# TensorE's instructions in the program's own order from step 40 of 128 on, and the last row tile of the last block in two PSUM banks

## The chip, the cores and the metric

The kernel runs on one core of one Trainium2 chip. The metric is the device time of one execution in microseconds (us). Engines are named as in the profile: PE is TensorE (PEld its weight loads), DVE is VectorE, ACT is ScalarE, POOL is GpSimd, SP issues most DMAs.

## The reference, cut to what matters

Input is a decayed linear attention over 2 sequences of 768 tokens with 8 heads of 64. Its output `x` (2 x 768 x 512) goes through two MLPs:

```python
X = fft(fft(x, axis=1), axis=2)
u = x + real(X)
un = (u - mean(u)) / sqrt(var(u) + 1e-6)
y = u + maximum(un @ w_ch1, 0) @ w_ch2          # 512 -> 2048 -> 512
yn = (y - mean(y)) / sqrt(var(y) + 1e-6) * g_ln
out = y + maximum(yn @ w2_ch1, 0) @ w2_ch2      # the second MLP, other weights
```

## The kernel before, in words

All matrix products of the two MLPs run in fp16 with every operand split into a high and a low part, three matmuls for one (`PASS`: high by high, high by low, low by high). Tokens are worked in four blocks of 384 (three row tiles of 128); the MLP's inner width 2048 in 16 slices of 128, called f. A **step** is one f of one block of one MLP: 128 steps, first MLP blocks 0, 1, 2, 3, second MLP blocks 0, 1, 3, 2. Step 40 is f = 8 of the first MLP's third block.

**One pair of steps** (`mlp_up_fast`, L800 to L855) computes two f at once by seven products of six matmuls with 192 columns (a Strassen-like scheme) into two PSUM banks, `ps_1...` (left) and `ps_2...` (right). I number them: products 1 to 3 in the even step (1 and 2 into the left bank, 3 into the right one), products 4 and 5 (left bank) in the odd step, products 6 (left) and 7 (right) at the end of the odd step (`rest`). Between them stand other engines' steps. After product 2, ACT copies m1 out (`s`, L831) and DVE adds it to product 2 (`s`, L832); product 4 writes the bank that this add reads, so it waits for it. After product 5, DVE forms u3 (`t`, L839) and adds it to the right bank (L840); products 6 and 7 follow. After them DVE adds (L845, L846), ACT makes the high half of `h` (L851) and DVE its low half (L852).

**The down pass** of step n works on f of step n - 3 (`mlp_down`, L877): for each of three row tiles j, three matmuls of 512 columns into a bank `ps_y` that collects all 16 f. In the program's order a pair of steps is: products 1, 2, 3; nine down matmuls; products 4, 5; nine down matmuls (these are the first that need the `h` of the pair before); products 6, 7.

**At the start of a block** products 2 and 3 need `th`, the sums of normalised inputs (`un_sums`, L774): two halves `kk`, each by six DVE adds (L779 to L787), an ACT cast (L794, high) and a POOL subtraction (L795, low). They are issued three steps and one step before the block, so the second half follows DVE's `t` of the last pair of the block before.

**Beside the products**, from about step 48 to 82, the second MLP's weights are converted (`conv_steps`, L280 to L325). For each of 32 tiles ACT makes `half` (L296) and copies it to a PSUM bank `ps_w` (L297), DVE joins it with the low bits (`wf`, L299), ACT scales by the gain (L320) and casts (L321), POOL subtracts (L323). Sums of these weights (`w1_sums`, L746 to L772: DVE, POOL, ACT, POOL) give `sw`, the operands of products 2, 3, 4, 6 and 7. PSUM has eight banks in three pools: "at" with three (`ps_w` and the right bank), "dn" with three (`ps_y`), "up" with two (the left bank).

**What sets the order.** A scheduler takes the program and decides in which order each engine's queue gets its instructions: it goes by the program's order and by a model of when operands are ready, and moves work forward where an engine would idle. Inside `manual_schedule` an engine's instructions keep the order in which the code issues them. Before, PE is manual in the prologue (up to the first MLP's first steps), and again in the last step (L1120 to L1122) and its end; in between the scheduler orders PE. DVE, ACT, POOL and SP are ordered by the scheduler in both kernels, around PE's order.

**The end** (`down_end`, L866): the last two f of the last block are done row tile by row tile, so that the first two tiles are added (L873) and stored (L874) while PE works on. The third row tile is done by halves of 256 columns, in the same bank: six matmuls for the left half, DVE's add of it, six for the right half.

Of the kernel before, what the change touches and what calls it, by code (L numbers as in the profile page):

```python
# [15 lines left out]
ALU = mybir.AluOpType  # L16
# [3 lines left out]
P = 128  # L20
B, H, S, D = 2, 8, 768, 64
DM, DF = 512, 2048
NCH = S // P
NK = DM // P
NF = DF // P
# [16 lines left out]
YS = 2.0 ** -15  # L42
# [10 lines left out]
EARLY0, GATEN, B1, SPC, DS, DC, DFO, DD, D1S, D2S, AO, YA, NR, NE, LN1, L1, L2, F01, F02, TL, R1, R2, SE, PR1, LAG, UB, FB, NW, MQ, SPL = 11, 8, 6, 2.0, 2.0, 5, 1.0, 0.5, 0.5, 1.0, "aba", "aa", 2, 0, 2, 2.5, 2.5, 16, 4, 3, 1.5, 2, "dddd_dppp", 0, 3, 3, 13, 11, 1, 3  # L53

SUMS = {(1, 0): 16, (1, 1): 18, (2, 0): 20, (2, 1): 25, (3, 0): 35, (3, 1): 38, (0, 0): 41, (0, 1): 43}

AWAY = {0: 37, 2: 39, 4: 41, 6: 43, 8: 45, 10: 47}

# [66 lines left out]
def tile_retention_fourier_mlp(ctx: ExitStack, tc: tile.TileContext, a: dict, out: bass.AP):  # L125
    nc = tc.nc
    pe, act, dve, pool, sp = nc.tensor, nc.scalar, nc.vector, nc.gpsimd, nc.sync
# [18 lines left out]
    def bank(which, name):  # L146
        return banks[which].tile([P, 512], F32, tag=which, name=name)

    def f32t(name, spare=None):
        if spare is not None:  # L150
            return wpool.tile([P, 512], F32, tag=f"w2_{spare}", name=name)
        return fp.tile([P, 512], F32, tag="f", name=name)
# [33 lines left out]
    U = [[ut[b][:, j] for j in range(6)] for b in range(B)]  # L186
# [16 lines left out]
    last = mask[:, :, 1:2].rearrange("p h one -> p (h one)")  # L203
# [653 lines left out]

    dn = {}

    def down_mm(m, blk, f, j, c=slice(0, DM)):  # L860
        h, w = hts[m, blk, f], w2t[m, f]
        for n, (x, y) in enumerate(PASS):
            pe.matmul(dn[blk][j][:, c], h[:, x, j * P:(j + 1) * P], w[:, y, c], start=f == 0 and n == 0,  # L863
                      stop=(f == NF - 1 or j == 2 and f == NF - 3) and n == 2, skip_group_check=j == 2)

    def down_end(m, blk):  # L866
        b, mir = divmod(blk, 2)
        for j in range(3):
            o = f32t(f"o{blk}_{j}")
            for c, eng in (((slice(0, DM), sp),) if j < 2 else ((slice(0, DM // 2), sp), (slice(DM // 2, DM), act))):  # L870
                for f in (NF - 2, NF - 1):
                    down_mm(m, blk, f, j, c)
                dve.scalar_tensor_tensor(o[:, c], dn[blk][j][:, c], YS, U[b][mir * 3 + j][:, c], op0=ALU.mult, op1=ALU.add)  # L873
                eng.dma_start(out[b, j * P:(j + 1) * P, c], o[:, c])  # L874

    def mlp_down(m, blk, f):
        if f == 0:  # L877
            dn[blk] = [bank("dn", f"ps_y{m}_{blk}_{j}") for j in range(3)]
        for j in range(3):
            down_mm(m, blk, f, j)  # L880
        if f < NF - 1:
            return
        b, mir = divmod(blk, 2)
        for j in range(3):
            u = U[b][mir * 3 + j]
            if m == 0:
                dve.scalar_tensor_tensor(u, dn[blk][j], YS, u, op0=ALU.mult, op1=ALU.add)  # L887
                continue
            o = f32t(f"o{blk}_{j}")
            dve.scalar_tensor_tensor(o, dn[blk][j], YS, u, op0=ALU.mult, op1=ALU.add)  # L890
            if not mir:
                sp.dma_start(out[b, j * P:(j + 1) * P, :], o)
                continue
            od = dram.tile([P, DM], F32, name=f"od{blk}_{j}")
            sp.dma_start(od, o)
            n0 = 1 if j == 0 else 0
            if n0:
                sp.dma_start(out[b, TB:TB + 1, :], od[0:1])
            ov, iv = out[b], od[:]
            hw = DM // 2  # L900
            sp.dma_start(bass.AP(ov.tensor, ov.offset + (S - P * j - n0) * DM, [[hw, 2], [-DM, P - n0], [1, hw]]),
                         bass.AP(iv.tensor, iv.offset + n0 * DM, [[hw, 2], [DM, P - n0], [1, hw]]))
# [83 lines left out]
    with tc.manual_schedule(engines={mybir.EngineType.PE, mybir.EngineType.DVE, mybir.EngineType.Pool, mybir.EngineType.Activation}):  # L986
        for z in ORDER.split():
# [3 lines left out]
            if z[0] == "W":  # L991
                ps = bank("up", f"warm{len(warm)}")
# [11 lines left out]
    def after(i, task):  # L1004
        with tc.issue_after(gates[i]):
            task()
# [9 lines left out]
    total = 2 * NB * NF  # L1016
    bg = {}
# [23 lines left out]
    n = t + DC + DFO  # L1041
# [46 lines left out]
    def step(n):  # L1088
        m = n // (NB * NF)
        return m, order[m][n // NF % NB], n % NF  # L1090
# [3 lines left out]
    for (m, blk), f in fast_from.items():  # L1094
        for kk in range(2):
            if m == 0 and blk < 3:
                put(16 * blk + f / 2 + kk - 3, lambda blk=blk, kk=kk: un_sums(0, blk, kk))
            else:
                at = m * NB * NF + order[m].index(blk) * NF
                put(at - TL + 2 * kk if (m, blk) != (1, 0) else at - 7 + 2 * kk, lambda m=m, blk=blk, kk=kk: un_sums(m, blk, kk))  # L1100
    for (g, kk), n in SUMS.items():
        put(n, lambda g=g, kk=kk: w1_sums(0, g, kk))

    def unit(n):
        rest = None
        if n < total:
            m, blk, f = step(n)
            if n >= SPL:
                rest = (mlp_up if f < fast_from.get((m, blk), NF) else mlp_up_fast)(m, blk, f)
        for _, _, task in sorted(bg.pop(n, ()), key=lambda z: z[0]):  # L1110
            after("dve", task) if n < GATEN else task()
        if n >= LAG:
            mlp_down(*step(n - LAG))
        if rest:
            rest()

    for n in range(total - 1):
        unit(n)
    assert not bg
    with tc.manual_schedule(engines={mybir.EngineType.PE}):  # L1120
        unit(total - 1)
        mlp_down(*step(total - LAG))  # L1122
        down_end(*step(total - 1)[:2])

# [24 lines left out]
```

## Time and profile before

| | |
|---|---|
| median of 3 runs | 590.84 us (590.81 to 591.52) |
| the profiled execution | 591.02 us, of which the span of its instructions is 589.2 |
| granted TensorE clock over the span | 0.999 |
| PE | busy 569.0 us (97% of the span), 4635 matmuls |
| DVE | 389.3 us (66%) |
| POOL | 280.9 us (48%) |
| ACT | 276.6 us (47%) |
| chain of work that ended last | PE 72%, DVE 10%, DMA 5%, ACT 5%, POOL 4%, issue 3% |

A matmul's duration in the profile holds its way through the array; matmuls follow each other closer than that, so the rate is read from start to start. Idle time of PE counts from the end of such a duration.

### The profile page before, as it was taken

What the parts mean: (1) busy time and instruction counts of PE and PEld (TensorE: products, weight loads), DVE (VectorE), ACT (ScalarE), POOL (GpSimd) and SP (SyncE); (2) the same over time, 40 slices, a digit from 0 to 9 for tenths busy, and PEclk for the clock granted to TensorE, in tenths of its full rate; (3) what the DMA queues carried; (4) which work ended last, traced back from release to release, by engine and by line L of the source; (5) the groups of instructions that cost most, each with busy time, mean ns of one, the idle gap of its engine ahead of it and who ended that gap; (6) DMA issues with size and microseconds to landing.
All of it is one profiled execution on the core that took longest, in us unless ns stands there. A gap on an engine that the chain in (4) does not pass through costs nothing.

```text
span 589.2 us, 11835 instructions
## 1 busy us (share of the span) xinstructions
PE 569.0 (97%) x4635; PEld 375.3 (64%) x4635; DVE 389.3 (66%) x870; ACT 276.6 (47%) x557; POOL 280.9 (48%) x294
## 2 busy tenths in 40 slices
PE   6889999999999999999999999999999999999997
PEld 4745645666554555666766676766767677767774
DVE  6898898667876449678777768766536453555333
ACT  3645789653233333465587787953223132322110
POOL 8925889976543564364466876953112100110000
PEclk9999999999999999999999999999999999999999
DMA  8995269861000011243265452500110025002001
GB/s 282 410 410 192 90 196 315 310 200 36 1 1 0 13 34 27 72 126 108 78 207 157 145 168 82 169 19 2 64 28 19 1 87 57 19 1 87 22 2 54
DMA packets 46470, 63.23 MB, mean 107 GB/s; under 512 B 26192, under 2 KB 28622, under 8 KB 46414
## 3 DMA queue, kind: packets, MB, share of 16 engines
q1 hardware_dynamic: 45598, 62.27, 33.4%
q8 instruction: 36, 0.59, 0.4%
q10 hardware_dynamic: 816, 0.21, 0.2%
q14 instruction: 20, 0.16, 0.1%
HBM read 52.23 MB, written 6.29 MB: 99 GB/s over the span
## 4 chain that ended last, share of the span: by engine, by line
PE 72%; DVE 10%; DMA 5%; ACT 5%; POOL 4%; issue 3%; SPq 0%; DVEq 0%; ACTq 0%; POOLq 0%
PE ps_y L863 35%; PE ps L819 22%; PE ps_h L726 10%; DMA kt<-in_kt 3%; POOL w L323 2%; PE ps_d L536 1%; DMA cdsd<-in_cd 1%; PE ps_s L361 1%; DMA u<-in_w 1%; ACT w L321 1%; DVE wr L759 1%; PE ps_i L403 1%; DVE u L887 1%; POOL sw L771 1%; ACT wf L320 1%
## 5 line engine op out<-in xcount | busy, mean ns | idle before, releaser
L863 PE MATMUL ps_y<-w,h 128*128 128x512 f16 x1158 | 280.3, 378 | 3.8 <-ACT h L851 1.6
L863 PEld LDWEIGHTS <-h 128*128 128x128 f16 x1158 | 109.4, 98 | 103.7 <-issue 4.5
L819 PEld LDWEIGHTS <-sw 128*128 128x128 f16 x1104 | 94.5, 98 | 17.0 <-issue 2.6
L819 PE MATMUL ps<-th,sw 128*128 128x192 f16 x828 | 92.0, 246 | 1.0 <-DVE wf L299 0.7
L819 PEld LDWEIGHTS <-w 128*128 128x128 f16 x828 | 71.9, 98 | 18.7 <-issue 0.2
L323 POOL TENSOR_TENSOR w<-wf,w 128x512 f16<-128x512 f32 x58 | 66.9, 1162 | 27.6 <-ACT w L321 27.5
L851 ACT ACTIVATE h<-ps 128x384 f16<-128x384 f32 x92 | 43.5, 489 | 71.7 <-DVE ps L845 67.3
L726 PE MATMUL ps_h<-unT,w 128*128 128x384 f16 x396 | 71.6, 326 | 0.1
L819 PE MATMUL ps<-unT,w 128*128 128x192 f16 x552 | 62.4, 246 | 0.0
L852 DVE SCALAR_TENSOR_TENSOR h<-ps,h 128x384 f16<-128x384 f32 x92 | 49.1, 554 | 14.2 <-ACT h L851 12.7
L726 PEld LDWEIGHTS <-w 128*128 128x128 f16 x396 | 37.9, 98 | 28.2 <-issue 0.5
L839 DVE TENSOR_TENSOR t<-ps,s 128x192 f32<-128x192 f32 x46 | 16.3, 354 | 51.1 <-PE ps L819 51.1
L771 POOL TENSOR_TENSOR sw<-ws,sw 128x512 f16<-128x512 f32 x32 | 37.3, 1182 | 20.8 <-ACT sw L770 20.8
L689 POOL TENSOR_TENSOR uns<-un,uns 128x512 f16<-128x512 f32 x21 | 25.2, 1201 | 39.6 <-ACT uns L688 39.6
L831 ACT COPY s<-ps 128x192 f32<-128x192 f32 x46 | 14.5, 315 | 61.5 <-PE ps L819 61.4
L668 POOL TENSOR_TENSOR rs<-rs,neghalf 128x1 f32<-128x1 f32 x24 | 14.3, 601 | 59.2 <-DVE rs L666 58.8
L321 ACT CAST w<-wf 128x512 f16<-128x512 f32 x58 | 35.2, 613 | 11.9 <-DVE wf L308 9.4
L795 POOL TENSOR_TENSOR th<-ts,th 128x384 f16<-128x384 f32 x24 | 22.1, 938 | 38.8 <-ACT th L794 38.8
L373 POOL TENSOR_TENSOR m<-m,m 128x512 f16<-128x512 f32 x24 | 31.6, 1335 | 4.3 <-ACT m L371 4.2
L845 DVE TENSOR_TENSOR ps<-ps,s 128x192 f32<-128x192 f32 x46 | 16.5, 360 | 25.2 <-PE ps L819 25.0
L741 DVE SCALAR_TENSOR_TENSOR h<-ps_h,h 128x384 f16<-128x384 f32 x36 | 19.8, 552 | 20.1 <-ACT h L740 20.0
L299 DVE SCALAR_TENSOR_TENSOR wf<-ws,ps_w 128x512 int32<-128x512 int32 x32 | 21.9, 686 | 14.8 <-ACT ps_w L297 8.8
(167 smaller groups left out, 834.4 us busy)
## 6 DMA issues: line engine op xcount, KB each, us to landing
ws<-in_w SPq DMA_DIRECT2D x25, 511.8 KB, 3.3
ws<-in_w2b SPq DMA_DIRECT2D x16, 511.8 KB, 4.0
ws<-in_w1b SPq DMA_DIRECT2D x16, 511.8 KB, 4.0
kt<-in_kt SPq DMA_DIRECT2D x12, 256.0 KB, 5.8
qt<-in_qt SPq DMA_DIRECT2D x12, 256.0 KB, 5.2
v<-in_v SPq DMA_DIRECT2D x12, 256.0 KB
k<-in_k SPq DMA_DIRECT2D x12, 256.0 KB, 5.1
pre<-in_w SPq DMA_DIRECT2D x4, 511.8 KB
```

The costliest lines, as they stand in the source:

```text
L299: dve.scalar_tensor_tensor(ti, raw[:, :, 0], 13, part.bitcast(I32), op0=ALU.logical_shift_right, op1=ALU.bitwise_or)
L321: act.copy(hi, t)
L323: (dve if m == 0 and i in (LD1 if kind == 1 else LD2) else pool).tensor_tensor(lo, t, hi, op=ALU.subtract)
L373: pool.tensor_tensor(t[:, 1], m32, t[:, 0], op=ALU.subtract)
L689: pool.tensor_tensor(s_[:, 1], un, s_[:, 0], op=ALU.subtract)
L726: pe.matmul(ps, w[:, i, k, fo:fo + P], x[:, j, k, :], start=n == 0, stop=n == 11)
L771: pool.tensor_tensor(lo, z, hi, op=ALU.subtract)
L795: pool.tensor_tensor(t[:, 1], z, t[:, 0], op=ALU.subtract)
L819: pe.matmul(ps, lhs, rhs, start=start and n == 0, stop=n == 5, skip_group_check=True)
L851: gate["relu"] = act.activation(hi, z, AF.Relu)
L852: dve.scalar_tensor_tensor(lo, z, 0.0, hi, op0=ALU.max, op1=ALU.subtract)
L863: pe.matmul(dn[blk][j][:, c], h[:, x, j * P:(j + 1) * P], w[:, y, c], start=f == 0 and n == 0, stop=(f == NF - 1 or j == 2 and f == NF - 3 ...
```

## The change

From step 40 on (`HAND`) all steps are issued inside `manual_schedule` for PE, so that PE's queue has the program's order up to the end. In the last block (second MLP, block 2) the third row tile gets two accumulators of 256 columns for the whole block, one in a bank of pool "dn" and one in a bank of pool "at"; each down pass of that block then has three matmuls of 256 columns for either instead of three of 512. `down_end` goes through the same list of parts. Nothing else is added or removed.

```diff
--- before.py
+++ after.py
@@ -53,6 +53,8 @@
 
+
+HAND = 40
 
 
@@ -857,37 +859,42 @@
 
     dn = {}
 
-    def down_mm(m, blk, f, j, c=slice(0, DM)):
+    WHOLE, LEFT, RIGHT = slice(0, DM), slice(0, DM // 2), slice(DM // 2, DM)
+
+    def down_mm(m, blk, f, part):
+        j, c, ps = part
         h, w = hts[m, blk, f], w2t[m, f]
         for n, (x, y) in enumerate(PASS):
-            pe.matmul(dn[blk][j][:, c], h[:, x, j * P:(j + 1) * P], w[:, y, c], start=f == 0 and n == 0,
-                      stop=(f == NF - 1 or j == 2 and f == NF - 3) and n == 2, skip_group_check=j == 2)
+            pe.matmul(ps, h[:, x, j * P:(j + 1) * P], w[:, y, c], start=f == 0 and n == 0, stop=f == NF - 1 and n == 2)
 
     def down_end(m, blk):
         b, mir = divmod(blk, 2)
-        for j in range(3):
-            o = f32t(f"o{blk}_{j}")
-            for c, eng in (((slice(0, DM), sp),) if j < 2 else ((slice(0, DM // 2), sp), (slice(DM // 2, DM), act))):
-                for f in (NF - 2, NF - 1):
-                    down_mm(m, blk, f, j, c)
-                dve.scalar_tensor_tensor(o[:, c], dn[blk][j][:, c], YS, U[b][mir * 3 + j][:, c], op0=ALU.mult, op1=ALU.add)
-                eng.dma_start(out[b, j * P:(j + 1) * P, c], o[:, c])
+        o = [f32t(f"o{blk}_{j}") for j in range(3)]
+        for part in dn[blk]:
+            j, c, ps = part
+            for f in (NF - 2, NF - 1):
+                down_mm(m, blk, f, part)
+            dve.scalar_tensor_tensor(o[j][:, c], ps, YS, U[b][mir * 3 + j][:, c], op0=ALU.mult, op1=ALU.add)
+            (act if c == RIGHT else sp).dma_start(out[b, j * P:(j + 1) * P, c], o[j][:, c])
 
     def mlp_down(m, blk, f):
         if f == 0:
-            dn[blk] = [bank("dn", f"ps_y{m}_{blk}_{j}") for j in range(3)]
-        for j in range(3):
-            down_mm(m, blk, f, j)
+            last = (m, blk) == step(total - 1)[:2]
+            dn[blk] = [(j, WHOLE, bank("dn", f"ps_y{m}_{blk}_{j}")) for j in range(2 if last else 3)]
+            if last:
+                dn[blk] += [(2, c, bank(z, f"ps_y{m}_{blk}_{z}")[:, :DM // 2]) for c, z in ((LEFT, "dn"), (RIGHT, "at"))]
+        for part in dn[blk]:
+            down_mm(m, blk, f, part)
         if f < NF - 1:
             return
         b, mir = divmod(blk, 2)
-        for j in range(3):
+        for j, _, ps in dn[blk]:
             u = U[b][mir * 3 + j]
             if m == 0:
-                dve.scalar_tensor_tensor(u, dn[blk][j], YS, u, op0=ALU.mult, op1=ALU.add)
+                dve.scalar_tensor_tensor(u, ps, YS, u, op0=ALU.mult, op1=ALU.add)
                 continue
             o = f32t(f"o{blk}_{j}")
-            dve.scalar_tensor_tensor(o, dn[blk][j], YS, u, op0=ALU.mult, op1=ALU.add)
+            dve.scalar_tensor_tensor(o, ps, YS, u, op0=ALU.mult, op1=ALU.add)
             if not mir:
                 sp.dma_start(out[b, j * P:(j + 1) * P, :], o)
                 continue
@@ -1114,11 +1121,12 @@
         if rest:
             rest()
 
-    for n in range(total - 1):
+    for n in range(HAND):
         unit(n)
-    assert not bg
     with tc.manual_schedule(engines={mybir.EngineType.PE}):
-        unit(total - 1)
+        for n in range(HAND, total):
+            unit(n)
+        assert not bg
         mlp_down(*step(total - LAG))
         down_end(*step(total - 1)[:2])
 
```

The tiles below carry the program's names and a number; line numbers of the changed kernel are two higher up to L857. First PE, at the start of the second MLP's third block (block 3); `ps_11_3_0` is the left bank of its first pair, `th0_1_3_0` and `th0_1_3_1` are the two halves of the sums, `ps_y1_1_0` is the down pass of the block before. Before:

```order
L819 MATMUL ps_11_3_0_6289<-unT1_3_5817,w1_1_0_4071 128x192
L819 LDWEIGHTS sw1_0_0_4110
L819 MATMUL ps_11_3_0_6289<-th0_1_3_0_6163,sw1_0_0_4110 128x192
L863 LDWEIGHTS h1_1_6_6192
L863 MATMUL ps_y1_1_0_5729<-w2_1_13_5454,h1_1_6_6192 128x512
```

With the change:

```order
L821 MATMUL ps_11_3_0_6291<-unT1_3_5819,w1_1_0_4073 128x192
L821 LDWEIGHTS sw1_0_0_4112
L821 MATMUL ps_11_3_0_6291<-th0_1_3_0_6165,sw1_0_0_4112 128x192
L821 LDWEIGHTS sw1_0_1_0_4284
L821 MATMUL ps_11_3_0_6291<-th0_1_3_1_6256,sw1_0_1_0_4284 128x192
```

What moved: product 2 is no longer broken off after its first matmul; its second one, which reads the second half of the sums, stands right behind.

Second DVE, between the pairs f = 6 and f = 8 of the first MLP's last block (block 3); `wf` are conversions, `h0_3_3` is what the pair f = 6 gives, `s0_3_8` and `t0_3_9` belong to the pair f = 8. Before:

```order
L840 TENSOR_TENSOR ps_20_3_6_4162<-ps_20_3_6_4162,t0_3_7_4204 128x192
L299 SCALAR_TENSOR_TENSOR wf2_1_3_4336<-ws2_1_3_4334,ps_w2_1_3_4338 128x512
L764 TENSOR_TENSOR ws12_1_0_1_4284<-wf1_1_1_4209,wf1_1_3_4273 128x256
L832 TENSOR_TENSOR s0_3_8_4248<-ps_10_3_8_4249,s0_3_8_4248 128x192
L845 TENSOR_TENSOR ps_10_3_6_4161<-ps_10_3_6_4161,s0_3_6_4160 128x192
L846 TENSOR_TENSOR ps_20_3_6_4162<-ps_20_3_6_4162,s0_3_6_4160 128x192
L852 SCALAR_TENSOR_TENSOR h0_3_3_4243<-ps_10_3_6_4161,h0_3_3_4243 128x2x192
L852 SCALAR_TENSOR_TENSOR h0_3_3_4243<-ps_20_3_6_4162,h0_3_3_4243 128x2x192
L299 SCALAR_TENSOR_TENSOR wf1_1_4_4398<-ws1_1_4_4396,ps_w1_1_4_4400 128x512
L839 TENSOR_TENSOR t0_3_9_4315<-ps_10_3_8_4249,s0_3_8_4248 128x192
```

With the change:

```order
L847 TENSOR_TENSOR ps_10_3_6_4163<-ps_10_3_6_4163,s0_3_6_4162 128x192
L301 SCALAR_TENSOR_TENSOR wf1_1_3_4275<-ws1_1_3_4273,ps_w1_1_3_4277 128x512
L848 TENSOR_TENSOR ps_20_3_6_4164<-ps_20_3_6_4164,s0_3_6_4162 128x192
L854 SCALAR_TENSOR_TENSOR h0_3_3_4245<-ps_10_3_6_4163,h0_3_3_4245 128x2x192
L766 TENSOR_TENSOR ws12_1_0_1_4286<-wf1_1_1_4211,wf1_1_3_4275 128x256
L301 SCALAR_TENSOR_TENSOR wf2_1_3_4338<-ws2_1_3_4336,ps_w2_1_3_4340 128x512
L834 TENSOR_TENSOR s0_3_8_4250<-ps_10_3_8_4251,s0_3_8_4250 128x192
L854 SCALAR_TENSOR_TENSOR h0_3_3_4245<-ps_20_3_6_4164,h0_3_3_4245 128x2x192
L841 TENSOR_TENSOR t0_3_9_4317<-ps_10_3_8_4251,s0_3_8_4250 128x192
```

What moved: the adds of the pair f = 6 and its left `h` stand ahead of `s0_3_8`, which now follows them and both conversions.

Third ACT, at the same block's pair f = 10, whose copy is `s0_3_10`; `h0_3_4` is what the pair f = 8 gives. Before:

```order
L321 CAST w1_1_1_4404<-wf1_1_4_4398 128x512
L296 ACTIVATE half2_1_5_4562<-ws2_1_5_4559 128x512
L831 COPY s0_3_10_4373<-ps_10_3_10_4374 128x192
L320 ACTIVATE wf1_1_6_4452<-wf1_1_6_4452,gcol_187 128x512
L794 CAST th0_1_0_0_4328<-ts12_1_0_0_4322 128x384
L321 CAST w1_1_1_4404<-wf1_1_6_4452 128x512
L794 CAST th1_1_0_0_4331<-ts34_1_0_0_4323 128x384
L851 ACTIVATE h0_3_4_4368<-ps_10_3_8_4249 128x2x192
L851 ACTIVATE h0_3_4_4368<-ps_20_3_8_4250 128x2x192
L297 CAST ps_w1_1_5_4552<-half1_1_5_4551 128x512
```

With the change:

```order
L299 CAST ps_w1_1_4_4402<-half1_1_4_4401 128x512
L796 CAST th0_1_0_0_4330<-ts12_1_0_0_4324 128x384
L853 ACTIVATE h0_3_4_4370<-ps_10_3_8_4251 128x2x192
L298 ACTIVATE half1_1_5_4553<-ws1_1_5_4550 128x512
L796 CAST th1_1_0_0_4333<-ts34_1_0_0_4325 128x384
L322 ACTIVATE wf1_1_4_4400<-wf1_1_4_4400,gcol_187 128x512
L299 CAST ps_w1_1_6_4456<-half1_1_6_4455 128x512
L833 COPY s0_3_10_4375<-ps_10_3_10_4376 128x192
L853 ACTIVATE h0_3_4_4370<-ps_20_3_8_4252 128x2x192
L323 CAST w1_1_1_4406<-wf1_1_4_4400 128x512
```

What moved: the two activations of `h0_3_4` stood behind `s0_3_10` and four steps of conversions and sums that follow it; now the left one stands ahead of `s0_3_10`, with four such steps between them, and the right one just behind it.

## Rows read from the trace of the kernel before

**Rows 1.** PE groups by form, 251.13 to 586.1 us: busy us, mean ns, idle us before.
```profile
L863 PE MATMUL ps_y<-w,h 128*128 128x512 f16 x815 | 198.9, 379 | 1.2 <-ACT h L851 1.2
L819 PE MATMUL ps<-th,sw 128*128 128x192 f16 x788 | 87.6, 246 | 1.0 <-DVE wf L299 0.7
L819 PE MATMUL ps<-unT,w 128*128 128x192 f16 x522 | 59.1, 246 | 0.0
L819 PE MATMUL ps<-th,w 128*128 128x192 f16 x270 | 30.1, 246 | 0.0
...
L863 PE MATMUL ps_y<-w,h 128*128 128x256 f16 x12 | 1.6, 272 | 0.5 <-DVE o L873 0.5
```

**Rows 2.** Chain that ended last, 571 to 576 us: start us, us, what.
```profile
571.63 2.06 PE ps L819 x25
573.69 1.94 PE ps_y L863 x9
```

**Rows 3.** Windows, PE alone: stretch, its length, busy us (count), granted clock, DMA.
```profile
280.00:340.00 60.00, 58.39 (x477) 1.00 0.49 149
340.00:400.00 60.00, 59.44 (x484) 1.00 0.35 103
400.00:580.00 180.00, 179.92 (x1463) 1.00 0.13 32
```

**Rows 4.** Timeline of PE, 320 to 326 us: its longest stop in these stretches.
```profile
320.60 0.66 PE L819 MATMUL ps<-unT,sw 128*128 128x192 f16 x6
...
324.83 1.47 PE L863 MATMUL ps_y<-w,h 128*128 128x512 f16 x6 [0.79 <-ACT h L851]
```

**Rows 5.** Timeline, PE at the end: start us, us, what.
```profile
579.39 5.35 PE L863 MATMUL ps_y<-w,h 128*128 128x512 f16 x27
585.26 0.81 PE L863 MATMUL ps_y<-w,h 128*128 128x256 f16 x6 [0.52 <-DVE o L873]
```

**Rows 6.** Timeline from 458.9 us, ahead of a block start.
```profile
458.94 2.10 PE L863 MATMUL ps_y<-w,h 128*128 128x512 f16 x9
459.14 0.36 DVE L839 TENSOR_TENSOR t<-ps,s 128x192 f32<-128x192 f32 x1 [1.83 <-PE ps L819]
...
461.15 0.35 DVE L785 TENSOR_TENSOR ts<-tr,ts 128x192 f32<-128x192 f32 x1
...
461.59 0.93 ACT L794 CAST th<-ts 128x384 f16<-128x384 f32 x2 [4.87 <-DVE ts L785]
462.18 1.78 POOL L795 TENSOR_TENSOR th<-ts,th 128x384 f16<-128x384 f32 x2 [5.47 <-ACT th L794]
```

**Rows 7.** Timeline, 280 to 286 us, ahead of the first MLP's last block.
```profile
280.64 0.35 DVE L839 TENSOR_TENSOR t<-ps,s 128x192 f32<-128x192 f32 x1
...
284.38 1.78 POOL L795 TENSOR_TENSOR th<-ts,th 128x384 f16<-128x384 f32 x2 [1.43 <-ACT th L794]
```

**Rows 8.** ACT groups by form, 300 to 395 us: busy us, mean ns, idle before.
```profile
L296 ACT ACTIVATE half<-ws 128x512 f16<-128x512 bf16 x22 | 14.9, 676 | 0.6 <-DMA ws<-in_w2b 0.4
L297 ACT CAST ps_w<-half 128x512 f32<-128x512 bf16 x23 | 13.5, 586 | 7.0 <-DVE h L852 5.5 <-DVE wf L299 1.3
L851 ACT ACTIVATE h<-ps 128x384 f16<-128x384 f32 x26 | 12.0, 487 | 4.9 <-DVE ps L845 4.9
L320 ACT ACTIVATE wf<-wf,gcol 128x512 f32<-128x512 f32 x15 | 10.9, 724 | 1.9 <-DVE wf L299 1.6
...
L831 ACT COPY s<-ps 128x192 f32<-128x192 f32 x12 | 3.7, 309 | 0.0
```

**Rows 9.** DVE groups by form, 300 to 395 us.
```profile
L299 DVE SCALAR_TENSOR_TENSOR wf<-ws,ps_w 128x512 int32<-128x512 int32 x23 | 15.8, 685 | 11.6 <-ACT ps_w L297 5.7 <-POOL sw L771 1.7 <-POOL ws L767 1.5
...
L832 DVE TENSOR_TENSOR s<-ps,s 128x192 f32<-128x192 f32 x12 | 4.2, 352 | 1.2 <-ACT s L831 1.2
```

**Rows 10.** Timeline, POOL, 381 to 389 us: the last weight sums of the second MLP.
```profile
385.39 2.27 POOL L771 TENSOR_TENSOR sw<-ws,sw 128x512 f16<-128x512 f32 x2
```

**Rows 11.** PE weight loads of the products, costliest groups: busy us, mean ns, idle before.
```profile
L819 PEld LDWEIGHTS <-w 128*128 128x128 f16 x828 | 71.9, 98 | 18.7 <-issue 0.2
```

## The prediction, made before the changed kernel was run

> **What bounds the kernel now.** I read the groups of PE first, then where its idle time lies, then who ends it. Scheduler and program agree up to 251.13 us, where PE's queue first differs; from there to the end the trace has 815 matmuls of 512 columns, 1848 of 192 (788, 522 and two alike groups of 270, one shown, count 1850; two of these began before the stretch) and 12 of 256 [rows 1]. Undisturbed, 25 matmuls of 192 columns take 2.06 us and nine of 512 take 1.94, so 82.4 and 215.6 ns from start to start [rows 2]; six of 256 end 0.81 us after the first starts and one lasts 272 ns, so (0.81 - 0.27) / 5 = 0.108 [rows 1, 5]. All of them back to back need 815 x 0.2156 + 1848 x 0.0824 + 12 x 0.108 = 329.3 us. From 251.13 to the last start, 0.54 after 585.26, plus 0.11, are 334.8 us [rows 5]. PE therefore loses about **5.4 us** behind the first difference, and no order of the same matmuls can win more. PE's granted clock is 1.00, the level of 2.4 GHz, throughout [rows 3], so nothing is to be had there.
>
> Where the 5.4 us lie: PE's idle time is next to nothing up to 280, 1.6 us up to 340, 0.6 up to 400, then 0.1 in 180 us [rows 3], and 0.5 at the end [rows 5]. The rest, some 2.5 us, is hidden in the pipelined ends of the matmuls, about 0.16 (0.246 - 0.082) at each stop [rows 1, 2]. So about 4 us go in the stretch of the weight conversions, 0.7 at the end, and little in the three blocks after 400. In the conversions PE stops for ACT's h, 1.2 us, and for DVE's wf, 0.7 us, which holds a PSUM bank that product 3 wants [rows 1]; the longest stop is 0.79 us at 324.83, for h [rows 4].
>
> **The change part by part.** *The end.* 27 matmuls start at 579.39, 21 of 512 and 6 of 256: they are through at 579.39 + 4.53 + 0.65 = 584.57, but the right half starts at 585.26, because DVE reads the left half in the same bank [rows 5]. In two banks the right half starts at once: -0.69. DVE is done with the left half when the right one's matmuls end, so its add and its store move up with it.
>
> *The split tile.* 14 down passes x 3 = 42 matmuls of 512 columns become 84 of 256: 84 x 0.108 - 42 x 0.2156 = 0.02; the 256 columns are known from twelve matmuls only, so 0 to 0.2. I take 0.1.
>
> *The stops in the conversions go.* In program order a pair's h is wanted 18 + 12 matmuls of 192 and nine of 512 after its product 7: 30 x 0.0824 + 1.94 = 4.4 us. At 324.83 product 7 of that pair, six matmuls from 320.60, had ended at 321.10, 3.7 us before (the scheduler had put less between them) [rows 4]: 4.4 covers that. Product 3 is issued after products 1 and 2 and not before the last pair's end, so the bank for which PE waited for wf [rows 1] is wanted later too. All 5.4 us are thus open to be won, and what follows is what the new order loses.
>
> *Starts of blocks.* Before, PE broke product 2 off after one matmul and did down work (the first order fence). Now the second half of the sums is wanted in program order. From the end of product 5, which is the start of nine down matmuls at 458.94, DVE's t follows at 459.14, the last add that th needs at 461.15, ACT's cast at 461.59 and POOL's subtraction from 462.18, two of them in 1.78, so the first until 463.09 [rows 6]: 4.15 us after 458.94. Program order puts nine down matmuls, products 6, 7, 1 and five matmuls of product 2 between: 1.94 + 23 x 0.0824 = 3.84 us. Waiting with some 0.06 us of signal: **0.37 us at each of the three later blocks of the second MLP, 1.1 together**. Nothing hides it, since PE has no other instruction in its queue. At the first MLP's last block the same chain took from 280.64 (t) to 284.38 + 0.9 = 285.3, 4.65 us instead of 3.95 after t, because DVE's adds and a conversion on POOL met [rows 7]: 1.1 us there. Its ends are 0.37 (undisturbed) and 2.
>
> *The wait for s.* DVE's s now stands behind the pair before and its conversions (the second fence). I count from the first matmul of pair f = 8: product 6 of the pair before ended 0.49 earlier, DVE's first add ends at about +0.07 (0.2 and 0.36 after it [rows 6]), ACT's h at 0.6, half at 1.3, the scaling at 2.0, ps_w at 2.6, ACT's copy at 2.9 [rows 8]; DVE's wf2_1_3 follows ps_w and ends at 3.3, its s at 3.65 [rows 9]. Product 4 wants that at 18 x 0.0824 + 1.94 = 3.42. Late by 0.2; with one more cast ahead (third fence, f = 10) by 0.5 to 0.8. Four pairs stand like this: f = 8 and 10 of that block, f = 0 and 10 of the next. These sums leave out that ACT's instructions overlap a little, so the low end is 0; the high end is 0.25 for each of twelve pairs, 3 us, when ACT is behind all the way. I take **1.0**.
>
> *The last weight sums.* POOL finished the first of the last sums at 386.5 [rows 10]; in the new order PE asks for it after 765 matmuls of 192 and 326 of 512: 251.13 + 63.0 + 70.3 = 384.4, plus the 1.9 or so that the waits above have cost by then. I take **0.3**; ends are 0 (the conversions move up with PE) and 2.1 (they keep their clock and PE has waited for nothing).
>
> **The sum.** 5.4 - 0.1 - 1.1 - 1.1 - 1.0 - 0.3 = 1.8 us less. The profiled execution took 591.02, which would become 589.2; it lies 0.18 over the median of 590.84, so the median becomes **589.0**. Something under 0.2%, 1.2 us, can't be told from no change here.
>
> A rule that speaks against the change: each of the 42 added matmuls brings a weight load of 98 ns [rows 11]. Here the 1848 matmuls of 192 columns all have such a load of their own and still follow each other after 82.4 ns [rows 2], less than the load alone; a load that nothing covers would add 42 x 0.098 = 4.1 us. The Trainium skill, page "TensorE: Matmul & The Clock Gate", section "The mechanism", has it that a weight load overlaps running matmuls only when it goes to another row group, and these are full loads. By that rule the 4.1 us would be paid; the trace disagrees.
>
> **The rivals.** *No change.* The conversions set the pace, not PE's order: ACT, DVE and POOL have the same work, and where PE no longer stops for h it stops for s. With 0.2 for each of twelve pairs, 2.4 instead of 1.0, the sum is 5.4 - 0.1 - 2.2 - 2.4 - 0.3 = 0.4, so 590.4. For it: DVE's s has already cost 1.2 us of waiting for ACT's copy [rows 9]. Against: h's were the longer stops, and they get 4.4 us.
>
> *Less is lost.* ACT and DVE overlap so that s is on time, the sums come early, and the first MLP's last block waits like the others: 5.4 - 0.1 - 1.1 - 0.4 = 3.8, so 587.0.
>
> *Slower.* The place is product 2 of f = 12 in the second MLP's first block. ACT takes h first now and conversions after it, and its ps_w waits for DVE's h: 5.5 us in 23 conversions already [rows 8]. If that wait doubles, the sums come at 386.5 + 5.5 = 392.0, when PE asks at 386.3: 5.7 us. Sum: 5.3 - 3.2 - 5.7 = -3.6, so 594.4. It decides from sums that come over 3 us later than now. Against: ACT is off the mark by less than 1 us at most places, and PE's stops, which held ACT up in turn (4.9 us for DVE's adds [rows 8]), get fewer.
>
> *The loads are not hidden*: 589.0 + 4.1 = 593.1. That the order is not what the change says can be ruled out; the fences show it.
>
> **How the numbers follow.** Forecast 0.48; less is lost 0.10; no change 0.32; sums too late 0.09; loads not hidden 0.01, since rows 2 exclude them but for another width. Faster by over 0.2% is the first two, 0.58; within 0.2% 0.32; slower 0.10. The range goes from 587.0 (the better case) to 590.9, which takes in the no-change case and half a microsecond; outside it are the two slow cases and some 0.05 more.
>
> **What would show it.** After: idle time of PE before product 2 with POOL's th as its end, some 0.4 us at about 398, 457 and 516 us and about 1 near 281; no stop for ACT's h and none for wf at product 3; single stops of 0.2 to 0.8 before product 4 for DVE's s between 310 and 385; 84 more matmuls of 256 columns at 0.11 us; the right half's first matmul 0.11 after the left half's last. Wrong would be: stops for h, stops of over 1 us for sw, or a longer spacing in the last block.

## The result, and the profile after

The changed kernel takes 597.26 us (median of five runs, 596.94 to 597.75) against 590.85 (590.81 to 591.52) of the kernel before: 6.4 us **slower**, ratio 1.0105 with an interval of 1.0093 to 1.0116. The prediction said 589.0, so the sign is wrong.

The page of the changed kernel, its span and TensorE's row:

```profile
span 595.5 us, 11929 instructions
PE 572.5 (96%) x4677; PEld 381.3 (64%) x4677; DVE 390.7 (66%) x870; ACT 273.8 (46%) x557; POOL 281.3 (47%) x294
```

42 matmuls more than the 4635 before, as expected. PE's groups by form behind the first difference, up to 592 us, which answer to [rows 1]:

```profile
L868 PE MATMUL ps_y<-w,h 128*128 128x512 f16 x773 | 182.5, 380 | 0.0
L821 PE MATMUL ps<-th,sw 128*128 128x192 f16 x786 | 80.6, 247 | 5.8 <-DVE s L834 4.5 <-POOL th L797 0.9 <-ACT th L796 0.2
...
L821 PE MATMUL ps<-unT,sw 128*128 128x192 f16 x270 | 29.6, 246 | 1.3 <-DVE ps L842 1.3
L868 PE MATMUL ps_y_dn<-w,h 128*128 128x256 f16 x48 | 7.7, 272 | 0.0
L868 PE MATMUL ps_y_at<-w,h 128*128 128x256 f16 x47 | 7.6, 273 | 0.0
```

The stops for `h` and for `wf` are gone, as forecast. In their place PE waits for `s` (4.5 us), for the add of `u3` (L842, 1.3 us, ahead of product 7) and for `th` (1.1 us). Idle time counts from a matmul's pipelined end; measured from start to start over the undisturbed spacing, which I call **excess**, a stop is some 0.17 us longer. The excess behind the first difference is 5.05 us before and 11.5 after:

| us of excess | before | after |
|---|---|---|
| `h`, `wf` | 2.9 | 0 |
| `s`, ahead of product 4 | 0.7 | 5.55 |
| `u3`, ahead of products 6 and 7 | 0.4 | 2.15 |
| `th`, at block starts | 0.3 | 2.05 |
| lower clock | 0 | 1.7 |
| the end | 0.68 | 0 |

The difference of 6.5, with 0.1 for the shorter matmuls, comes within 0.2 us of the 6.4 measured. The windows (stretch, its length, PE busy and matmuls, granted clock, DMA) show the worst place, answering to [rows 3]:

```profile
324.00:326.00 2.00, 1.44 (x7) 1.00 0.16 23
326.00:328.00 2.00, 0.12 (x2) 0.99 0.72 231
328.00:330.00 2.00, 2.00 (x13) 0.50 0.61 219
330.00:332.00 2.00, 2.00 (x7) 0.65 0.13 51
332.00:334.00 2.00, 2.00 (x22) 1.00 0.22 20
```

PE stands still for 2.43 us, then its clock is at the lower of its two levels (0.50, 1.2 GHz) for 3.4 us, until about 331.4 (0.65 over the window from 330 is 1.4 us at 0.50). This is pair f = 10 of the first MLP's last block. Its timeline (start, us, engine, what; idle before):

```profile
317.97 2.64 POOL L325 TENSOR_TENSOR w<-wf,w 128x512 f16<-128x512 f32 x2
319.06 1.98 DVE L781 TENSOR_TENSOR tr<-unT 128x384 f32<-128x384 f16 x2
320.58 2.70 POOL L773 TENSOR_TENSOR sw<-ws,sw 128x512 f16<-128x512 f32 x2
321.22 1.04 DVE L786 TENSOR_TENSOR ts<-tr 128x192 f32<-128x192 f32 x1
322.18 1.31 DVE L788 TENSOR_TENSOR ts<-tr,tr 128x192 f32<-128x192 f32 x1
323.42 0.34 DVE L787 TENSOR_TENSOR ts<-tr,ts 128x192 f32<-128x192 f32 x1
323.80 0.51 ACT L796 CAST th<-ts 128x384 f16<-128x384 f32 x1 [3.64 <-DVE ts L787]
324.21 0.48 ACT L853 ACTIVATE h<-ps 128x384 f16<-128x384 f32 x1
326.70 0.33 ACT L833 COPY s<-ps 128x192 f32<-128x192 f32 x1
327.48 0.35 DVE L834 TENSOR_TENSOR s<-ps,s 128x192 f32<-128x192 f32 x1
327.88 1.06 PE L821 MATMUL ps<-th,sw 128*128 128x192 f16 x6 [2.43 <-DVE s L834]
```

Read it upwards from the last row. `s` is late because ACT's copy is late; ACT had stood idle 3.64 us for DVE's sums, with `h` and four more steps queued behind that cast; and DVE's sums took 1.04 and 1.31 us where the next one, alike, took 0.34. While they ran, POOL was subtracting. This holds throughout: from 250 to 560 us, 13 of DVE's adds of two operands in SBUF (the sums of inputs and of weights) took over 1.4 times their own length, and each of the 13 began while a two-operand step of POOL was running and ended 0.21 to 0.42 us after that step. The groups of the same adds, first 250 to 400 us, where POOL converts, then 400 to 560, where it hardly works (count, busy us, mean ns):

```profile
L781 DVE TENSOR_TENSOR tr<-unT 128x384 f32<-128x384 f16 x10 | 9.1, 954 | 0.3 <-DMA unT<-uns 0.3
L788 DVE TENSOR_TENSOR ts<-tr,tr 128x192 f32<-128x192 f32 x4 | 2.3, 586 | 0.0
```

```profile
L781 DVE TENSOR_TENSOR tr<-unT 128x384 f32<-128x384 f16 x11 | 5.7, 552 | 0.0
L788 DVE TENSOR_TENSOR ts<-tr,tr 128x192 f32<-128x192 f32 x6 | 2.1, 351 | 0.0
```

The same instruction (L781) took 954 ns on average here and 552 there.

The end went as predicted (timeline, answering to [rows 5]): the right half starts 0.65 us after the left one, that is with no stop, and both are added and stored in turn.

```profile
590.83 0.82 PE L868 MATMUL ps_y_dn<-w,h 128*128 128x256 f16 x6
591.48 0.82 PE L868 MATMUL ps_y_at<-w,h 128*128 128x256 f16 x6
```

### The profile page after: what moved, and what is told of

Same layout as the page of the kernel before. It is cut to its first block, busy times and chain, and to the rows that moved or that the text cites. A ratio compares the mean times of both kernels' runs of the same rounds, so it can differ in the third digit from the quotient of the medians.

```text
span 595.5 us, 11929 instructions
## 1 busy us (share of the span) xinstructions
PE 572.5 (96%) x4677; PEld 381.3 (64%) x4677; DVE 390.7 (66%) x870; ACT 273.8 (46%) x557; POOL 281.3 (47%) x294
## 4 chain that ended last, share of the span: by engine, by line
PE 35%; issue 9%; DVE 5%; POOL 3%; ACT 3%; DVEq 0%; POOLq 0%; ACTq 0%
PE ps L821 17%; PE ps_y L868 17%; POOL th L797 2%; DVE tr L781 1%; PE ps_y_dn L868 1%; PE ps_y_at L868 1%; ACT h L853 1%; ACT half L298 0%; ACT th L796 0%; DVE ts L788 0%; POOL uns L691 0%; DVE ws L766 0%; DVE ts L786 0%; POOL ws L767 0%; DVE ps L842 0%
## 5 line engine op out<-in xcount | busy, mean ns | idle before, releaser
L868 PE MATMUL ps_y<-w,h 128*128 128x512 f16 x1104 | 262.4, 380 | 2.1 <-ACT w L323 1.1
L868 PEld LDWEIGHTS <-h 128*128 128x128 f16 x1200 | 115.0, 98 | 111.1 <-issue 4.4
L821 PE MATMUL ps<-th,sw 128*128 128x192 f16 x828 | 85.4, 247 | 5.8 <-DVE s L834 4.5
L821 PE MATMUL ps<-unT,w 128*128 128x192 f16 x552 | 61.1, 247 | 0.0
L796 ACT CAST th<-ts 128x384 f16<-128x384 f32 x24 | 12.0, 508 | 52.1 <-DVE ts L787 41.3
L821 PE MATMUL ps<-unT,sw 128*128 128x192 f16 x276 | 30.3, 246 | 1.3 <-DVE ps L842 1.3
```

The costliest lines, as they stand in the source:

```text
L821: pe.matmul(ps, lhs, rhs, start=start and n == 0, stop=n == 5, skip_group_check=True)
L868: pe.matmul(ps, h[:, x, j * P:(j + 1) * P], w[:, y, c], start=f == 0 and n == 0, stop=f == NF - 1 and n == 2)
```

## The experiments

Times of a run stand against the kernel before in the same job, 591.12 us for the first four and the last four, 591.19 for the four between.

**1 to 4. Where is the time lost?** Only the step from which program order holds is changed. In run 1 it is the last one, so that the scheduler's order and the two banks are left; in runs 2, 3 and 4 the line reads 64 (the second MLP's first step), 48 (the first MLP's last block) and 88 (behind all conversions).

```diff
-HAND = 40
+HAND = 127
```

> TensorE's order is again the scheduler's up to the last step; only the two accumulators of the last row tile stay. Theory A (the time is lost where TensorE, in fixed order, stands in front of one late operand, each stop on its own, and two banks save the stop at the end): 590.85 - 0.68 + 0 to 0.1 = 590.2. Rival B (the two banks are what costs, by their 84 shorter matmuls or by the bank that they take from the other work): over 591.5.

Measured 590.80, ratio 0.9997 (0.9988 to 1.0005): no difference that can be told. It is 0.6 over theory A's number, of which 0.3 is the kernel before's higher time in this job; rival B is out. The trace has the 0.68 us at the end gone, but a stop of 0.40 us excess is new in the last block, where the scheduler had other down matmuls to place (and a smaller one, 0.24, at 323 us):

```profile
534.02 0.39 PE L868 MATMUL ps_y<-w,h 128*128 128x512 f16 x1 [0.24 <-DVE h L854]
```

> Program order from the second MLP's first step on (64 instead of 40). Theory A adds up the losses by place, as start-to-start excess over the ideal spacing: behind step 64 the changed kernel lost 0.52 + 0.24 + 0.31 + 0.37 + 0.37 = 1.8 us, the kernel before 0.59 + 0.30 + 0.22 + 0.19 + 0.68 = 2.0; so 590.6, and only that. Rival C (other engines fall behind wherever TensorE is in program order while weights are converted): conversions go on to step 82, so 2 us or more, over 592.5.

Measured 591.23, ratio 1.0004 (0.9995 to 1.0013); the excess is 4.9 us, against 5.05 before. Theory A; rival C is out: conversions go on to step 82 here, and program order beside them alone is not slow.

> Program order from the first MLP's last block on (48 instead of 40). Theory A: behind step 48 the changed kernel lost 6.5 us more up to step 64 where the kernel before lost 2.4, so 590.6 + 4.1 = 594.7, with the stop of 2.4 us ahead of product 4 of pair f = 10 and the lower clock behind it still there. Rival D (ScalarE and VectorE come into the last block with a backlog that program order made in steps 40 to 47): without that backlog the stop shrinks to below 1 us, the clock stays at its full level, and the time is below 592.

Measured 596.95, ratio 1.0100 (1.0086 to 1.0114). The stop ahead of product 4 of pair f = 10 is there unchanged, 2.42 us of idle time, with the lower clock, although the steps 40 to 47 are the scheduler's: no backlog, rival D is out. The time is 2.2 us over theory A's; at the seam of the two orders the profiled execution has a new stop of 1.43 us (for `th`, its sums late again), with a stretch at 0.50 behind it.

> Program order from step 88 on, after all conversions. Theory A: of the changed kernel's losses only the two later block starts remain, 0.37 + 0.37, against 0.68 of the kernel before at the end: 590.85 + 0.06 = 590.9 (0 to 0.1 for the shorter matmuls not counted). By rival C the same. If program order cost nothing at block starts, 590.2.

Measured 591.15, ratio 1.0004 (0.9995 to 1.0013), as theory A has it. With run 2, the loss lies in steps 40 to 63.

**5. Is the lower clock the stop's doing?**

```diff
-HAND = 40
+HAND = 88
+
+STOPS = {(1, 1, 10): 7, (1, 1, 14): 9, (1, 3, 4): 11, (1, 3, 8): 13, (1, 3, 12): 16, (1, 2, 4): 20}
...
-            dve.tensor_tensor(u2, left[:, HB:TB], m1, op=ALU.add)
+            for _ in range(1 + STOPS.get((m, blk, f), 0)):
+                dve.tensor_tensor(u2, left[:, HB:TB], m1, op=ALU.add)
```

> The kernel of the run from step 88 on, with VectorE's add of s repeated 7, 9, 11, 13, 16 and 20 times more (the same result each time) in six pairs of the second MLP that lie two or more pairs apart, after all conversions. In a quiet pair s is there 1.38 us before product 4 wants it and a repeat takes 0.27 us, so TensorE is to stop for about 0.5, 1.1, 1.6, 2.1, 2.9 and 4.0 us, 12.2 in all: 591.15 + 12.2 = 603.4 if a stop costs only its length. Theory E (the lower clock behind the stop of 2.4 us of the changed kernel comes of the stop itself): the stops of 2.4 us and more are followed by a stretch at a granted clock of about 0.5 that costs some 1.7 us each, so about 606.8, and the shorter ones show where it begins. Rival F (it came of what else ran in that place, conversions and transfers): the clock stays at 1.00 throughout and the time is 603.4.

Measured 619.26, 28.1 us over the kernel before and over run 4, from whose kernel this one starts. The repeats came out longer than I had set (about 0.39 us each), so the stops of the profiled execution had an excess of 1.3, 2.4, 2.9, 3.7, 4.8 and 6.4 us, 21.6 in all. In that execution (620.67 us, 29.5 over run 4's profiled one) the lower clock adds 8.3, some 1.7 behind each of the five longer ones ((1 - 0.66) x 5 us in the last row here), and one wait of 0.4 at a block start is gone. Windows around the three shortest:

```profile
442.00:444.00 2.00, 1.23 (x6) 1.00 0.10 24
444.00:446.00 2.00, 1.61 (x15) 1.00 0.19 41
459.00:461.50 2.50, 0.27 (x2) 0.99 0.00 0
461.50:464.00 2.50, 2.47 (x14) 0.50 0.00 0
464.00:466.00 2.00, 2.00 (x9) 0.78 0.00 0
...
488.00:493.00 5.00, 4.89 (x25) 0.66 0.14 48
```

After 1.16 us of idle time the clock stayed at 1.00, after 2.27 it fell to 0.50, with no conversion and no transfer beside it (DMA 0.00). The stop by itself is enough: theory E; rival F is out.

**6. Do the sums in ACT's queue make the stop?**

```diff
-                put(at - TL + 2 * kk if (m, blk) != (1, 0) else at - 7 + 2 * kk, ...
+                put(at - TL + 2 * kk if (m, blk) != (1, 0) else at - 11 + 2 * kk, ...
```

> The changed kernel, but the sums of the inputs of the second MLP's first block are issued four steps earlier (eleven and nine steps ahead of the block instead of seven and five), so that ScalarE's queue no longer has a cast that waits for them ahead of the h and the s of pair f = 10. Theory A: the stop of 2.6 us there becomes one like its neighbour's (0.9), the clock stays at its full level (1.7 saved), and one of the earlier pairs may lose up to 0.9: 593.9, between 593.0 and 595.0. Rival D (VectorE and ScalarE are behind by a backlog of conversions, whatever stands where): a stop of over 2 us stays in that stretch with the lower clock behind it, and the time is over 596.

Measured 596.83, ratio 1.0101 (1.0087 to 1.0114): neither theory's number. The stop at pair f = 10 is gone, and one of 2.06 us of idle time has come at pair f = 6, where the sums stand now, with 1.05 ahead of product 7 behind it. It follows the sums, so that their one place in the queue is not the cause. They took long here too, where POOL works: L786 took 1.06 us, L788 0.88 and a weight sum (L766) 1.38.

```profile
306.94 1.16 POOL L325 TENSOR_TENSOR w<-wf,w 128x512 f16<-128x512 f32 x1 [1.61 <-ACT w L323]
...
307.25 1.06 DVE L786 TENSOR_TENSOR ts<-tr 128x192 f32<-128x192 f32 x1
...
308.86 1.27 POOL L325 TENSOR_TENSOR w<-wf,w 128x512 f16<-128x512 f32 x1
309.04 1.38 DVE L766 TENSOR_TENSOR ws<-wf,wf 128x256 f32<-128x256 f32 x1
...
313.58 0.66 PE L821 MATMUL ps<-th,sw 128*128 128x192 f16 x6 [2.06 <-DVE s L834]
```

The clock stayed at 1.00 behind 2.06 us.

**7. Sums one step earlier, from step 64 on.**

```diff
-HAND = 40
+HAND = 64
...
-                put(at - TL + 2 * kk if ...
+                put(at - TL - m + 2 * kk if ...
```

> The run from step 64 on, with the sums of the three later blocks of the second MLP issued one step earlier. Theory A: the waits for the second half of the sums at those block starts, 0.31 + 0.37 + 0.37 us, go and nothing comes in their place: 591.23 - 1.05 = 590.2, that is 1.0 under the kernel before's 591.1 when taken in the same job (the excess over the ideal spacing falls from 4.9 to 3.8 us). Rival: the sums now hold up the adds of the pairs before the blocks, and the time stays within 0.3 us of 591.2.

Measured 591.65, ratio 1.0009 (1.0000 to 1.0018), neither theory's number. The three waits are gone, but one of 1.24 us (1.4 of excess) is new, at product 6 of the last pair ahead of the second MLP's second block, and its timeline gives the cause:

```profile
393.81 1.03 DVE L781 TENSOR_TENSOR tr<-unT 128x384 f32<-128x384 f16 x2 [2.06 <-DMA unT<-uns]
...
396.35 0.66 PE L821 MATMUL ps<-th,w 128*128 128x192 f16 x6 [1.24 <-DVE t L841]
```

The sums, now ahead of `t` in DVE's queue, waited 2.06 us for the transfer that brings their input. (Run 12's expectation says of this wait that DVE's sums met POOL's conversions. This row refutes it: two adds in 1.03 us is their own length. POOL's part lies one step earlier: it ended the transfer's input, `uns`, at 391.37, behind conversions and weight sums, and the transfer was issued at 391.39.)

**8. More time for `s`, less for `u3`.** The rest of the edit lets `mlp_down` take a part of its row tiles.

```diff
+        ahead = n >= HAND and n % 2 == 1
+        if ahead:
+            mlp_down(*step(n - LAG), slice(None, 1))
...
-            mlp_down(*step(n - LAG))
+            mlp_down(*step(n - LAG), *[slice(1, None)] * ahead)
```

> The changed kernel, but from step 40 on three of the nine down matmuls behind product 5 (the first row tile) are put ahead of product 4 (program order changed, nothing added). That gives s 0.65 us more and u3 0.65 us less. Theory A: each stop for s gets 0.65 shorter where it is longer than that (0.6, 0.9, 0.4, 2.6, 0.9, 0.2 at present), with the stop at pair f = 10 below the length at which the clock fell, each of the five stops ahead of product 6 up to 0.65 longer: 597.3 - 2.9 - 1.7 + 3.2 = 595.9, between 593.5 and 596.5. Rival D (the other engines need their time whatever TensorE's order): 597 to 597.5 with the lower clock still there.

Measured 599.76, ratio 1.0150 (1.0136 to 1.0163), slower than any theory had it. PE's waits from 251 us on:

```profile
PE ps L821 <- DVE ps L842: 5.2, 6, 1.9
PE ps L821 <- POOL th L797: 2.0, 4, 0.5
PE ps L821 <- ACT th L796: 2.0, 4, 0.5
```

No stop for `s` over 0.1 us is left, and none at the lower clock, but those ahead of product 7 (the expectation calls it product 6) went from 1.3 to 5.2, and those for `th` from 1.1 to 4.0: I had left out that the sums at block starts follow product 5 too and lose the same 0.65 us, at both halves. The waits were moved here, and grew.

**9 to 11. POOL's subtractions out.** In run 9 three of them, in run 10 all of the second MLP's conversions and of the weight sums from step 40 on, in run 11 the same in the kernel before. In their place POOL only fills with zeros, so the low halves of those weights and sums are left out. The edit of run 9; in runs 10 and 11 the conditions are the second MLP (`m == 1`) and a step from 40 on.

```diff
-        (dve if ... else pool).tensor_tensor(lo, t, hi, op=ALU.subtract)
+        if (kind, m, i) == (2, 1, 3):
+            pool.memset(lo, 0.0)
+        else:
+            (dve if ... else pool).tensor_tensor(lo, t, hi, op=ALU.subtract)
...
-            pool.tensor_tensor(lo, z, hi, op=ALU.subtract)
+            if (m, g, kk) == (1, 0, 1):
+                pool.memset(lo, 0.0)
+            else:
+                pool.tensor_tensor(lo, z, hi, op=ALU.subtract)
```

> The changed kernel, in which three of GpSimd's 128x512 subtractions, those that overlap VectorE's sums of the inputs at 319 to 324 us, only fill their result with zeros; the low halves of one weight tile and of one group of weight sums are left out by that. TensorE's, VectorE's and ScalarE's orders are the same. Theory G (VectorE's adds that read both operands from SBUF are held up while GpSimd reads SBUF; there the six adds took 5.1 us, elsewhere 0.55 and 0.34 each, 2.5 in all): the stop ahead of product 4 of pair f = 10 shrinks from 2.6 us to under 0.5, the clock behind it stays at 1.00 (1.7), the wait of 0.35 ahead of product 7 at 321 us goes: 597.26 - 2.3 - 1.7 - 0.3 = 593.0, between 592.5 and 594. Rival D (the queues' orders alone make the stop, with their conversions ahead of s): a stop of 2 us or more stays, and the time with it, 596.5 to 597.5.

Measured 594.41, ratio 1.0051 (1.0037 to 1.0065), 2.85 us less than the changed kernel. The queues of PE, DVE and ACT hold the same instructions in the same order; only three of POOL's steps differ. The fills have no operand to wait for and ran earlier (at 295, 301 and 312 us), so that beside these sums POOL had one subtraction left, from 319.20 to 320.36, and then nothing until 323.00:

```profile
320.29 1.02 DVE L787 TENSOR_TENSOR tr<-unT 128x384 f32<-128x384 f16 x2
321.49 0.35 DVE L792 TENSOR_TENSOR ts<-tr 128x192 f32<-128x192 f32 x1
321.76 0.35 DVE L794 TENSOR_TENSOR ts<-tr,tr 128x192 f32<-128x192 f32 x1
322.41 0.51 ACT L802 CAST th<-ts 128x384 f16<-128x384 f32 x1 [1.00 <-DVE ts L793]
324.23 2.11 PE L874 MATMUL ps_y<-w,h 128*128 128x512 f16 x9
...
326.46 0.66 PE L827 MATMUL ps<-th,sw 128*128 128x192 f16 x6
```

The sums are back at their own length, the stop went from 2.43 us to 0.12 (the nine down matmuls end at 326.34, product 4 starts at 326.46), and the clock behind it stays up. That is theory G. The time is 0.4 over its range's upper end; the next pair's stop grew from 0.76 to 1.69 us.

> The same for all of GpSimd's subtractions in the second MLP's weight conversions and in the weight sums from step 40 on (their low halves are left out); TensorE's order is that of the changed kernel. Theory G: of the 5.5 us of stops for s, the 2.2 ahead of product 7 and the 1.7 of the lower clock at most 2 are left, and of the 2.0 us at block starts some 1.7: 597.26 - 7.7 = 589.6, between 588.5 and 591, no slower than the kernel before. Rival D: the stops for s stay for the most part, over 595.

Measured 588.77, ratio 0.9962 (0.9950 to 0.9974): 8.5 us less than the changed kernel, PE's order untouched. Theory G. Its waits:

```profile
PE ps L828 <- POOL th L804: 0.6, 3, 0.2
PE ps L828 <- DVE ps L849: 0.3, 1, 0.3
PE ps L828 <- DVE s L841: 0.2, 1, 0.2
```

POOL is also done sooner here, and a few of DVE's and ACT's steps stand in another order, so some of the gain may come of that; run 9, with three steps, is the clean case.

> The kernel before with the same steps left out. The scheduler then puts TensorE's instructions in another order from the middle of the last block of the first MLP on. Theory G': the scheduler's order already hid most of the hold-up, since it put other matmuls where s was late; there are 5.05 us to be lost at all, of which 0.7 at the end stay, so it gains 0 to 2 us: 589 to 591, and program order and the scheduler's order then come within 1.5 us of each other. Rival: the gain is as large as in the changed kernel (5 us or more), so under 587.

Measured 587.53, ratio 0.9941 (0.9928 to 0.9953): 3.6 us less, more than I allowed for and less than half of the changed kernel's gain. POOL's subtractions thus cost program order 8.5 us and the scheduler's order 3.6 (with an order that the scheduler made anew). Without them program order is still the slower one by 1.2: its four block starts cost 1.4 in run 10 (0.38 + 0.32 + 0.37 + 0.37 of excess), and run 11 has no stop there, but still the 0.7 at the end.

**12. What can be kept.**

```diff
-HAND = 40
+HAND = 64
...
-                put(at - TL + 2 * kk if ...
+                put(at - TL - (m and blk > 1) + 2 * kk if ...
```

> Program order from step 64 on, with the sums issued one step earlier for the last two blocks alone. The run with all three blocks earlier lost its three waits at block starts (1.05 us) and got one of 1.4 us in the first block, where VectorE's sums met GpSimd's conversions. Theory G: without conversions beside them nothing is held up: the excess over the ideal spacing falls from 4.9 us (from step 64 on, sums as before) to 4.15, so 0.9 us under the kernel before plus 0.1 for the shorter matmuls, about 590.3 where that takes 591.1. Rival: a wait of 0.5 us or more appears in the pairs before these two blocks too, and the time is not under the kernel before's.

Measured 590.32, ratio 0.9986 (0.9977 to 0.9995), 0.8 us under the kernel before: the only kernel here that leaves nothing out and is faster, clear of noise, than both the kernel before and the changed one. Theory G. Excess 4.3 us; nothing is waited for in the last two blocks.

## Why the prediction was wrong, step by step

- **Right.** The 5.4 us to be won (its own terms, 334.8 less 329.3, give 5.5; 5.05 as stops); no stop for `h` or for `wf`; the end (0.69 predicted, 0.68 gone); the split tile (its matmuls of 256 columns stand 109 ns apart, 0.1 us in all; no weight load shows); the later block starts (0.37 each predicted, 0.31, 0.37 and 0.37 measured) and the first MLP's last one (1.1 predicted, 0.99 measured). The weight sums `sw` (0.3) made no wait at all.
- **The step that failed** is "The wait for s": 1.0 us taken, 5.55 measured, beyond even its upper end of 3. It counted ACT's and DVE's steps ahead of `s` one by one with durations from groups of one form, as if each engine had only its own work. Run 9 shows what was left out: DVE's adds of two operands in SBUF are held up while POOL subtracts, and `s` stands behind them. The trace before showed it: at the start of the first MLP's last block I saw that "DVE's adds and a conversion on POOL met" [rows 7], priced that one place rightly, and did not ask at which other places the same adds stand ahead of something that PE wants. Only one of the four pairs that I counted agreed, f = 10 of the first MLP's last block: the waits were at f = 10, 12 and 14 of the block before (1.8 us, where weight sums and the staged conversions run already), f = 10 and 12 of the last block (3.5) and f = 8 of the next (0.24). The place that I saw, in the kernel before (L784 alone takes 0.35):

```profile
281.45 1.49 POOL L323 TENSOR_TENSOR wst<-wf,wst 128x512 f16<-128x512 f32 x1 [3.00 <-ACT wst L321]
...
282.11 1.05 DVE L784 TENSOR_TENSOR ts<-tr 128x192 f32<-128x192 f32 x1
```

- **Two terms were missing.** The wait ahead of product 7 for DVE's add of `u3` (L842, 2.15 us) comes from the same hold-up (in run 10, without POOL's subtractions, 0.5 of it is left): in program order nine down matmuls and product 6 are all the cover that this add has. And the lower clock behind the long stop cost 1.7 us; I had read [rows 3] as "nothing to be had there", which was true of a gain and not of a loss.
- **The rivals.** "No change" had the right mechanism, PE stops for `s` where it stopped for `h`, at less than half the size. "Slower" named the wrong place: the sums `sw` were never late.
- **Why the scheduler's order bears it better.** Both kernels have these hold-ups (from 250 to 400 us the first of these adds took 712 ns on average before, against 552 from 400 us on); run 11 prices them at 3.6 us there. Program order makes PE stand in front of whichever operand comes late, and in run 8 shifting its work only shifted the wait. That the scheduler does better because it mixes other matmuls in where `s` or `u3` is due I read from the two orders; no run shows it by itself.

The Trainium skill, page "SBUF — State Buffer", section "Who interferes with whom", states what the runs found: a DVE instruction with two SBUF inputs contends with a GpSimd instruction that reads SBUF, not with one that only writes it, and the later one blocks until the first is done. The trace agrees: L788 ended at 322.18 + 1.31 = 323.49, 0.21 us after the second of POOL's subtractions (320.58 + 2.70 = 323.28), and beside zero fills, which only write, a like add of run 10 (L796, which is L789 of the changed kernel) took 0.35:

```profile
326.37 0.99 POOL L326 MEMSET w<- 128x512 f16 x2 [2.55 <-PE ps L828]
...
326.79 0.35 DVE L796 TENSOR_TENSOR ts<-tr,ts 128x192 f32<-128x192 f32 x1
```

## What to carry to other kernels

A fixed order on the busiest engine turned every late operand into a stop here; before fixing it, list for each point what must be ready, and take the durations of the engines that make it where their neighbours are at work, not from a mean. An add of two SBUF operands on VectorE beside GpSimd's subtractions took three times as long (1.04 us against 0.34), and a stop of 2.4 us was followed by a stretch at half clock that cost another 1.7. Where the other engines were quiet, program order cost nothing (runs 2 and 4), and operands issued a step earlier made it pay (run 12) where their own input was there in time (in run 7 it was not).

## What the runs showed of the hardware that was not expected

- TensorE's granted clock: 1.00 behind single stops of 0.76, 1.16 (run 5), 1.91 (run 8) and 2.06 us (run 6) of idle time, 0.50 for 3.4 us behind stops of 2.27 us and more, and also behind 1.43 us that followed another stop of 0.43 two us before (run 3). A longer stop did not cost more: 1.7 us behind 2.27 of idle time, (1 - 0.63) x 5 = 1.85 behind 6.26, where the clock had fallen within the stop already (0.74 over the 6 us before).
- These are single profiled executions, and the lower clock did not come every time. Two of run 3's four executions have a mean clock of 0.997 instead of 0.993 or 0.994 and took 596.2 us instead of 597.7 and 598.0; two of run 5's have 0.986 instead of 0.983 and took 618.6 on average instead of 620.2. As an estimate from these numbers, that is one such stretch fewer (0.003 x 617 us is 1.9, and one stretch costs some 1.7).
- VectorE's adds beside GpSimd's subtractions: 954 ns against 552, single ones 1.31 us against 0.35. The other way round, a subtraction of GpSimd (128x512) took 1.53 us in the changed kernel where one of these adds had begun just before it (319.06 and 319.09 us), against 1.16 by itself.
- The profiled executions of runs 1, 6, 7 and 9 have a stretch at 0.50 within their first 36 us, ahead of all that these kernels change. One stop for `h` of 0.40 us that all the kernels have stands at 249.05 us in the kernel before, and at 249.49, 249.95, 249.87 and 250.06 in these four: differences of half a microsecond to one lie in their single times. The two of run 9's five executions with a clock of 1.000 took 593.8 and 593.9 us, within its theory's range.
